# Attention on one core: normalization one query tile later, transposes two and the product with V three tiles behind the scores

## The chip, the cores and the metric

The kernel runs on one core of one Trainium2 chip. The metric is the device time of one execution in microseconds, as the median of several executions; lower is better.

## What is computed

The reference is causal attention with a second, linear "memory" part, followed by two dense blocks without bias. Cut to what matters:

```
B, H, S, D = 4, 8, 576, 64
scores = q @ k.T / sqrt(D); scores[j > i] = -1e9
a      = exp(scores - scores.max(-1)); a /= a.sum(-1) + 1e-9
local  = a @ v
q_p    = phi(q)                         # q+1 where q>0, else exp(q)
mem    = (q_p @ M_prev) / (q_p . z_prev + 1e-6)
x      = sigmoid(beta) * mem + (1 - sigmoid(beta)) * local     # (2304, 512)
x      = ((x @ w1) * (x @ w2)) @ w3 @ w_out                    # d_ff 1024
h      = x @ w_in                                              # d_ff 2048
out    = (h - tanh(h)) @ w_out2
```

The weights arrive as 64-bit numbers; the kernel loads the raw words and decodes them on the chip to float32, and then splits each into a high and a low part for TensorE (three matmuls in place of one).

## The kernel before

**Attention.** 32 heads are taken as 16 pairs P. Each pair has five query tiles u: four of 128 rows and a fifth of 64 rows in which both heads share the 128 partitions. That makes 80 tiles, n = 0 to 79, with n = 5P + u. A tile goes through five steps, each a function:

- S, `scores` and `rmax`: the score matmuls of the causal part (width 128(u+1); 288 twice for u = 4) and the mask matmuls on TensorE into a PSUM tile `sc`, of which there are two; then the row maximum on VectorE (L337) into the small tile `st`.
- E, `exps`: the exponential on ScalarE (L346) with its row sum; it frees the `sc` tile.
- N, `norm`: 1e-9 is added (L355) and the reciprocal is taken (L356) on VectorE, then the rows are scaled on GpSimd (L363).
- T, `trans`: the scaled rows are transposed on TensorE, block by block (L395, L402, L406), and copied out of PSUM to the `g` tiles (L374 on ScalarE or L376 on VectorE).
- A, `av`: for u = 1 and u = 4 the product with V, `o<-g,v` on TensorE; the result is copied to `xs`. After u = 4 the V of the pair after next is loaded (L189).

Two more letters stand in the loop: L loads and scales the next pairs' q and k, and G runs background work: first `fold_work`, the product of w3 and w_out, in 16 groups of 12 matmuls `fo` whose operands are decoded by a chain of steps (L74 on ScalarE; L75, L77, L81, L84 on VectorE; L96 and L99 on GpSimd); the two halves of a result are added on VectorE (L257) and split (L259 on ScalarE, L260 on VectorE). After the folds come the first w1 and w2 tiles (`wa`, `wb`) and the memory part (`mem_tok`: tiles `mw` with L490, L491, L493, L494, L497 and so on, transposes L506, product `mo`, sum L523).

**What sets the order.** A loop over m calls the steps in the order of the string ORDER, each for tile m minus its lag:

```python
ORDER = "SENTLGA"
for m in range(NU + 8):
    for x in ORDER:
        do(x, m - LAG[x])
```

This is the order of issue. A scheduler then lays the instructions of each engine in a row, with its own estimates of when each could start, and the order of issue counts where several could go. So each engine's row differs from the order of issue, and a lag moves what may be chosen rather than a fixed place. Each engine then runs its row in order. Buffers are given in the order of issue.

**After attention.** The tiles of attention are given back (`att.close()`), and new pools take their place, among them the one that holds w1 and w2 from the third pair on. Then six groups g of 384 tokens go through the first dense block: `ab<-xh,wa` and `ab<-xh,wb` (24 matmuls for each of eight slices f), ScalarE and VectorE (L646, L647, L650, L651), and `x<-abh,wf`. The decoding of the remaining weights and the rest of the memory part run beside the first groups. The second dense block (`h`, `o<-...,gh`) ends the kernel.

Of the kernel before, what the change touches and what calls it, by code (L numbers as in the profile page):

```python
# [32 lines left out]
def block_kernel(ctx, tc, qk, qt, vt, mp, zp_d, beta, w1, w2, w3t, wo, wi, wo2, ident_d, mask_d, out):  # L33
# [104 lines left out]
    def run(gen):  # L138
        for _ in gen:
            pass  # L140
# [17 lines left out]
    DW = 1  # L158
    HIP = 1
    ORDER = "SENTLGA"  # L160
    LAG = {'S': 0, 'E': 0, 'N': 0, 'T': 1, 'L': 0, 'G': 3, 'A': 2}
    WI = ()
    PO_, PA = "xzw", "r1234"
    OP, FL = 5, "V"
# [99 lines left out]
    if True:  # L264
# [170 lines left out]
        N = 384  # L435
# [135 lines left out]
        def do(x, n):  # L571
            if not 0 <= n < NU:
                return
            P, u = units[n]
            if x == "S":
                scores(n)
                rmax(n)
            elif x == "E":
                exps(n)
            elif x == "N":  # L580
                norm(n)
            elif x == "T":
                trans(n)
            elif x == "A" and u in (1, 4):
                av(P, u // 4)
                if u == 4 and P + 2 < 16:
                    load_v(P + 2)
            elif x == "L":
                if u == 0 and 1 <= P <= 16 - RB:
                    load_qk(P + RB - 1)  # L590
                if u == 2 and P < 15:
                    scale_q(P + 1)
            elif x == "G":
                bgc[0] += BG if n < MB else BG2
                with ExitStack() as s:
                    for e, k in TH:
                        if n - k >= 0:
                            s.enter_context(tc.issue_after(mark[e][n - k]))
                    while bgc[0] >= 1:
                        if next(bg, None) != 1:  # L600
                            bgc[0] -= 1
# [4 lines that stand above are left out]
        run(bg)  # L606
# [308 lines left out]
def build(nc, arrays):  # L915
    args = []
    for name, a in arrays.items():
        args.append(nc.dram_tensor(f"in_{name}", a.shape, mybir.dt.from_np(a.dtype), kind="ExternalInput").ap())
    o = nc.dram_tensor("out_0", (_N, 512), F32, kind="ExternalOutput").ap()
    with tile.TileContext(nc, schedule_with_timeline_sim=True) as tc:  # L920
        block_kernel(tc, *args, o)
# [40 lines left out]
```

## Time and profile before

| | |
|---|---|
| median of 3 executions | 1037.43 us (1036.61 to 1040.4) |
| the profiled execution's own time | 1034.81 us |
| its span, first to last instruction | 1033.0 us |
| TensorE busy | 984.2 us (95%) |
| VectorE busy | 745.9 us (72%) |
| ScalarE busy | 594.7 us (58%) |
| GpSimd busy | 361.8 us (35%) |
| mean granted TensorE clock | 0.990 |

A busy share is an average over stages with different limits: the attention tiles run from the start to about 275 us, the first dense block from there to about 620 us, the second to the end. Which engine limits a stage is read from that stage.

### The profile page before, as it was taken

How to read it: one execution, taken by the hardware profiler on the slowest of the kernel's cores; microseconds unless marked ns; L12 is line 12 of the kernel's file. 1: busy time of each engine (PE TensorE's matmuls, PEld its weight loads, DVE VectorE, ACT ScalarE, POOL GpSimd, SP SyncE). 2: the span in 40 equal slices, each digit the busy share in tenths (PEclk: the TensorE clock that was granted, in tenths of full speed). 3: DMA queues.
4: the chain of work that ended last, by engine and by line, in shares of the span. 5: the costliest groups of instructions: out<-in, count | busy, mean ns of one | idle time of the engine just before them, and what ended most of it. 6: DMA issues, size and time to landing. Idle time of an engine off the chain costs nothing.

```text
span 1033.0 us, 15587 instructions
## 1 busy us (share of the span) xinstructions
PE 984.2 (95%) x5512; PEld 826.1 (80%) x5512; DVE 745.9 (72%) x1361; ACT 594.7 (58%) x1356; POOL 361.8 (35%) x396
## 2 busy tenths in 40 slices
PE   5999999889988989999999979999999999999998
PEld 2565566545777878999999979999999999989996
DVE  5858787787599996475212497778787887788775
ACT  4767766577433433233222546777686676777765
POOL 3656655585466213200000573322222222222221
PEclk9999999999999999999999998999999999999999
DMA  6434543242145552143000010000000000000000
GB/s 206 158 113 128 177 139 98 97 144 88 42 135 156 160 184 81 34 134 109 1 1 1 1 62 1 1 1 31 1 32 1 1 32 1 29 4 1 32 1 31
DMA packets 44238, 68.27 MB, mean 66 GB/s; under 512 B 4865, under 2 KB 30209, under 8 KB 44161
## 3 DMA queue, kind: packets, MB, share of 16 engines
q1 hardware_dynamic: 44160, 67.29, 20.4%
q8 instruction: 43, 0.70, 0.3%
q14 instruction: 35, 0.28, 0.1%
HBM read 62.56 MB, written 4.72 MB: 65 GB/s over the span
## 4 chain that ended last, share of the span: by engine, by line
PE 79%; DVE 11%; issue 3%; DMA 3%; ACT 2%; POOL 2%; SPq 0%; DVEq 0%; ACTq 0%; POOLq 0%
PE o L143 24%; PE h L143 20%; PE ab L143 14%; PE x L143 7%; PE sc L143 6%; PE fo L143 4%; PE t L395 3%; DVE T L81 2%; DVE T L75 2%; DVE st L337 1%; PE mo L143 1%; DVE T L77 1%; ACT p L346 1%; DMA raw<-in_wi 1%; DVE T L84 1%
## 5 line engine op out<-in xcount | busy, mean ns | idle before, releaser
L849 POOL TENSOR_TENSOR gl<-s,gh 128x384 fp32r<-128x384 f32 x96 | 100.8, 1050 | 292.3 <-ACT gh L843 281.7
L363 POOL TENSOR_SCALAR p<-p,st 128x128 f32<-128x128 f32 (+2 forms) x144 | 94.5, 669 | 63.4 <-DVE st L356 32.3
L143 PE MATMUL x<-abh,wf 128*128 128x384 f32 x384 | 109.1, 345 | 5.6 <-ACT abh L650 5.6
L143 PE MATMUL ab<-xh,wa 128*128 128x384 f32 x384 | 109.3, 342 | 4.4 <-POOL wa L99 2.1
L143 PE MATMUL ab<-xh,wb 128*128 128x384 f32 x384 | 108.3, 340 | 3.1 <-POOL wb L96 2.0
L825 DVE SCALAR_TENSOR_TENSOR s<-s,u 128x384 f32<-128x384 f32 x96 | 81.9, 853 | 21.8 <-ACT s L815 20.7
L143 PE MATMUL sc<-r 64*64 64x288 f32 (+4 forms) x384 | 79.6, 480 | 17.5 <-ACT p L346 11.7
L346 ACT ACTIVATE p<-sc,st 128x128 f32<-128x128 f32 (+2 forms) x144 | 78.3, 549 | 29.8 <-DVE st L337 25.1
L647 DVE TENSOR_TENSOR a<-ab,a 128x384 f32<-128x384 f32 x48 | 26.4, 551 | 86.3 <-PE ab L143 73.5
L74 ACT ACTIVATE T<-raw 128x512 f32<-128x512 f32 x72 | 48.6, 674 | 62.3 <-DMA raw<-in_wi 11.9
L821 ACT ACTIVATE u<-u,pc 128x384 f32<-128x384 f32 x96 | 59.3, 619 | 43.4 <-DVE s L825 43.3
L337 DVE TENSOR_REDUCE st<-sc 128x2 f32<-128x256 f32 (+4 forms) x80 | 64.1, 803 | 26.6 <-PE sc L143 26.2
L831 DVE TENSOR_TENSOR t<-h,t 128x384 f32<-128x384 f32 x96 | 53.3, 555 | 38.8 <-ACT t L814 38.5
L143 PEld LDWEIGHTS ab<-xh,wa 128*128 128x128 f32 x384 | 70.3, 188 | 9.0 <-issue 3.1
L143 PEld LDWEIGHTS x<-abh,wf 128*128 128x128 f32 x384 | 71.3, 192 | 7.1 <-ACT abh L650 6.5
L143 PEld LDWEIGHTS ab<-xh,wb 128*128 128x128 f32 x384 | 71.1, 190 | 4.6 <-POOL wb L96 2.8
L813 ACT ACTIVATE u<-h 128x384 f32<-128x384 f32 x96 | 47.0, 490 | 48.0 <-PE h L143 48.0
L143 PE MATMUL x<-abl,wf 128*128 128x384 f32 x192 | 67.0, 349 | 5.5 <-DVE abl L651 5.5
L830 DVE SCALAR_TENSOR_TENSOR s<-s,s 128x384 f32<-128x384 f32 x96 | 61.0, 635 | 8.1 <-DVE s L825 0.5
L143 PE MATMUL ab<-xl,wa 128*128 128x384 f32 x192 | 65.1, 339 | 0.0
L143 PE MATMUL ab<-xl,wb 128*128 128x384 f32 x192 | 64.7, 337 | 0.0
L837 DVE COPY_PREDICATED s<-u,t 128x384 f32<-128x384 uint32 x96 | 58.6, 610 | 8.3
(218 smaller groups left out, 2579.5 us busy)
## 6 DMA issues: line engine op xcount, KB each, us to landing
raw<-in_wo SPq DMA_DIRECT2D x24, 512.0 KB, 3.5
r<-in_qk SPq DMA_DIRECT2D x15, 576.0 KB, 4.1
raw<-in_w3t SPq DMA_DIRECT2D x16, 512.0 KB, 3.7
raw<-in_w SPq DMA_DIRECT2D x16, 512.0 KB, 3.7
raw<-in_wi SPq DMA_DIRECT2D x16, 512.0 KB, 3.8
v<-in_vt SPq DMA_DIRECT2D x16, 320.0 KB, 3.1
mw<-in_qt SPq DMA_DIRECT2D x18, 256.0 KB, 2.9
out<-ob SPq DMA_DIRECT2D x18, 256.0 KB, 2.3
```

The costliest lines, as they stand in the source:

```text
L74: AC.activation(out=tf, in_=hw.bitcast(F32), func=AF.Abs)
L143: return PE.matmul(o, lhsT, rhs, start=start, stop=stop).ins
L337: mark["V"][n] = DV.tensor_reduce(out=st[:, 0:2] if u < 4 else st[:, 0:1], in_=seen(n), axis=AX.X if u < 4 else AX.XY, op=ALU.max, negate= ...
L346: mark["A"][n] = AC.activation(out=p[:, x], in_=sc[:, x], func=AF.Exp, bias=st[:, x.start:x.start + 1], accum_out=st[:, 2 + x.start:3 + x. ...
L363: (DV if NV[u] == "V" else PO).tensor_scalar(out=pr, in0=pr, scalar1=sc, scalar2=1.0, op0=ALU.mult, op1=ALU.mult)
L813: AC.activation(out=u, in_=o, func=AF.Square)
L821: AC.activation(out=u, in_=u, func=AF.Relu, bias=pc[:, 2:3])
L825: DV.scalar_tensor_tensor(out=s1, in0=s1, scalar=k2[0], in1=u, op0=ALU.add, op1=ALU.mult)
L830: DV.scalar_tensor_tensor(out=s1, in0=s2, scalar=k2[1], in1=s1, op0=ALU.add, op1=ALU.mult)
L831: DV.tensor_tensor(out=t, in0=o, in1=t, op=ALU.subtract)
L837: DV.copy_predicated(out=s1, mask=u[:].bitcast(U32), data=t)
L849: PO.tensor_tensor(out=l, in0=s1, in1=h[:].bitcast(F32), op=ALU.subtract)
```

## The change

One line differs: the lags of N, T and A each grow by one. Normalization of a tile is issued one step after its scores and exponential, the transposes two steps after, and the product with V three steps after. The lags of the loads and of the background work stay.

```diff
     ORDER = "SENTLGA"
-    LAG = {'S': 0, 'E': 0, 'N': 0, 'T': 1, 'L': 0, 'G': 3, 'A': 2}
+    LAG = {'S': 0, 'E': 0, 'N': 1, 'T': 2, 'L': 0, 'G': 3, 'A': 3}
```

Every engine runs the same instructions as before, in the same number. Of TensorE's 5178 rows the first 78 (to the mask of tile 7 and a few transposes) and the last 3387 (from inside the first dense block on) stand in the same order as before; in between tiles trade places. Two places show how.

**Place A, the end of the last fold.** On VectorE, around the sum L257 of the last fold, before (the reduction at the end is that of tile 57; `sc_2209` is its score tile, `sc_2146` that of tile 56):

```order
L257 TENSOR_TENSOR s_2178<-fo_2165,wf7p_1356 128x512
L337 TENSOR_REDUCE st_2151<-sc_2146 128x2
L493 SCALAR_TENSOR_TENSOR mw_2184<-mw_2184 128x512
L81 SCALAR_TENSOR_TENSOR T_2193<-raw_2187,T_2193 128x512
L260 TENSOR_TENSOR wf7_2180<-s_2178,wf7_2180 128x512
L337 TENSOR_REDUCE st_2214<-sc_2209 128x2
```

and after the change (`sc_2187` is tile 57, `sc_2225` tile 58):

```order
L257 TENSOR_TENSOR s_2169<-fo_2156,wf7p_1335 128x512
L260 TENSOR_TENSOR wf7_2171<-s_2169,wf7_2171 128x512
L337 TENSOR_REDUCE st_2192<-sc_2187 128x2
L81 SCALAR_TENSOR_TENSOR T_2207<-raw_2180,T_2207 128x512
L497 TENSOR_REDUCE mst_2310<-mw_2175 128x8
L376 COPY g1_2082<-t_2147 128x8x64
L337 TENSOR_REDUCE st_2230<-sc_2225 128x2
```

The reduction of tile 56, a step of the memory part and a decode step no longer stand between the last fold's sum and the reduction of tile 57. On TensorE, from the last matmuls of that fold on, before (128x256 is tile 56, 128x384 tile 57):

```order
L143 MATMUL fo<-wb_1408,zs 128x512 x3
L143 MATMUL sc<-r 128x256 x2
L143 LDWEIGHTS identb
L143 MATMUL sc<-maskb,identb 128x128
L143 LDWEIGHTS identb
L143 MATMUL sc<-maskb,identb 128x128
L143 MATMUL sc<-r 128x384 x2
```

and after (128x512 is tile 58):

```order
L143 MATMUL fo<-wb_1399,zs 128x512 x3
L143 MATMUL sc<-r 128x384 x2
L143 LDWEIGHTS identb
L143 MATMUL sc<-maskb,identb 128x128
L395 MATMUL t<-ident,p 128x128 x4
L143 LDWEIGHTS identb
L143 MATMUL sc<-maskb,identb 128x128
L143 MATMUL sc<-r 128x512 x2
```

The last fold moved behind the scores of tile 56, one tile later. The first fold moved likewise, behind the scores of tile 10 in place of tile 9.

**Place B, the end of attention.** On TensorE the last product with V, `o<-g,v`, before (the `ab` matmuls are the first two slices of the dense block, and 12 of them stand behind the product, ahead of the transposes L506):

```order
L143 MATMUL ab<-xh,wb_2653 128x384 x2
L143 MATMUL ab<-xl,wb_2653 128x384
L143 MATMUL ab<-xh,wb_2653 128x384
L143 MATMUL o<-g_2884,v_102 64x320 x6
L143 MATMUL o<-g_2884,v_102 64x192 x2
L143 MATMUL o<-g_2885,v_102 64x64 x2
L143 MATMUL ab<-xh,wa_2391 128x384
L143 MATMUL ab<-xl,wa_2391 128x384
```

and after:

```order
L143 MATMUL ab<-xh,wb_2640 128x384
L143 MATMUL ab<-xl,wb_2640 128x384
L143 MATMUL ab<-xh,wb_2640 128x384
L143 MATMUL o<-g_2894,v_102 64x320 x6
L143 MATMUL o<-g_2894,v_102 64x192 x2
L143 MATMUL o<-g_2895,v_102 64x64 x2
L143 MATMUL mo<-ident,mw 128x128 x4
```

All 48 `ab` matmuls of the two slices now stand ahead of the last product. On ScalarE the copy of that product, `xs<-o,omgt` of 128x5x64, before:

```order
L374 ACTIVATE xs_1685<-o,omgt 128x5x64
L646 ACTIVATE a<-ab 128x384 x2
L650 ACTIVATE abh<-a 128x384
L374 ACTIVATE mq_1534<-mo 128x2x128
L74 ACTIVATE T<-raw 128x512
```

and after:

```order
L646 ACTIVATE a<-ab 128x384 x2
L650 ACTIVATE abh<-a 128x384 x2
L374 ACTIVATE xs_1717<-o,omgt 128x5x64
L374 ACTIVATE mq_1513<-mo 128x2x128
L74 ACTIVATE T<-raw 128x512
```

The steps of the first two slices moved ahead of the copy; the next decode step L74 stays behind both.

## Rows read from the trace of the kernel before

**Rows 1.** Windows by stage: busy us (instructions) by engine, granted clock, DMA share, GB/s.
```profile
30.00:200.00 170.00, 167.17 (x1068) 100.46 (x1067) 126.81 (x276) 115.47 (x319) 100.27 (x134) 1.00 0.40 126
200.00:275.00 75.00, 66.69 (x465) 38.63 (x466) 57.89 (x138) 50.41 (x141) 46.15 (x60) 0.98 0.32 104
275.00:400.00 125.00, 111.33 (x621) 98.08 (x621) 111.10 (x206) 45.43 (x90) 50.66 (x42) 0.96 0.46 144
400.00:600.00 200.00, 200.00 (x1166) 196.20 (x1165) 88.60 (x166) 64.90 (x133) 28.36 (x24) 1.00 0.15 44
```

**Rows 2.** Timeline of all engines, 194 to 222: start, duration, instruction, [idle before].
```profile
194.81 0.69 DVE L257 TENSOR_TENSOR s<-fo,wf7p 128x512 f32<-128x512 f32 x1 [0.72 <-PE fo L143]
...
195.54 0.63 ACT L259 ACTIVATE wf<-s 128x512 fp32r<-128x512 f32 x1 [0.46 <-DVE s L257]
195.56 0.92 PE L143 MATMUL sc<-r 64*128 64x384 f32 x4
...
197.04 1.65 POOL L494 TENSOR_TENSOR mw<-mw,mc 128x512 f32<-128x512 f32 x1 [2.06 <-DVE mw L493]
...
197.50 1.75 DVE L260 TENSOR_TENSOR wf<-s,wf 128x512 fp32r<-128x512 f32 x1
197.53 1.13 PE L143 MATMUL sc<-r 64*128 64x512 f32 x4 [0.28 <-ACT p L346]
...
198.71 0.39 PE L395 MATMUL t<-ident,p 128*128 128x128 f32 x2
...
199.17 0.94 DVE L337 TENSOR_REDUCE st<-sc 128x2 f32<-128x768 f32 x1
...
200.78 0.57 ACT L346 ACTIVATE p<-sc,st 128x384 f32<-128x384 f32 x1
...
201.49 1.19 PE L143 MATMUL sc<-r 64*64 64x288 f32 x8 [2.40 <-ACT p L346]
...
202.74 4.11 PE L143 MATMUL o<-g,v 128*64 128x320 f32 x20
```

**Rows 3.** The window behind that wait, columns as in rows 1.
```profile
201.50:206.70 5.20, 5.20 (x29) 2.47 (x29) 4.81 (x13) 1.66 (x5) 2.82 (x5) 0.67 0.52 153
```

**Rows 4.** Chain that ended last: a product of the same 20 matmuls, later.
```profile
234.84 2.35 PE o L143 x20
```

**Rows 5.** Instructions of L260: duration ns min/median/max, first and last start.
```profile
L260 DVE TENSOR_TENSOR wf<-s,wf x8: 677/722/1748, 140.2 to 197.5; 128x512 fp32r<-128x512 f32 x8
```

**Rows 6.** Timeline of TensorE at the end of attention.
```profile
275.62 2.42 PE L143 MATMUL o<-g,v 128*64 128x320 f32 x20
277.97 0.45 PE L143 MATMUL ab<-xh,wa 128*128 128x384 f32 x1
...
279.99 0.33 PE L143 MATMUL ab<-xh,wb 128*128 128x384 f32 x1
```

**Rows 7.** Timeline of GpSimd, same stretch.
```profile
278.22 0.62 POOL L96 TENSOR_SCALAR wa<-T 128x512 fp32r<-128x512 f32 x1 [4.39 <-PE o L143]
```

**Rows 8.** Timeline of ScalarE, same stretch.
```profile
278.09 0.53 ACT L374 ACTIVATE xs<-o,omgt 128x320 f32<-128x320 f32 x1 [4.69 <-PE o L143]
...
281.08 0.65 ACT L74 ACTIVATE T<-raw 128x512 f32<-128x512 f32 x1
```

**Rows 9.** Timeline of VectorE, same stretch.
```profile
279.39 0.56 DVE L647 TENSOR_TENSOR a<-ab,a 128x384 f32<-128x384 f32 x1 [5.15 <-ACT a L646]
...
282.61 0.41 DVE L75 TENSOR_SCALAR T<-T 128x512 f32<-128x512 f32 x1
282.94 0.55 DVE L651 TENSOR_TENSOR abl<-a,abh 128x384 fp32r<-128x384 f32 x1
...
283.74 0.41 DVE L490 TENSOR_SCALAR mw<-mw 128x512 f32<-128x512 f32 x1
```

**Rows 10.** Waits of VectorE, 255 to 400: us in total, times, longest.
```profile
DVE mw L490 <- DMA mw<-in_qt: 6.5, 4, 3.0
```

**Rows 11.** DMA issues of the page: times, KB each, us to landing.
```profile
v<-in_vt SPq DMA_DIRECT2D x16, 320.0 KB, 3.1
```

**Rows 12.** Transposes of TensorE: duration ns min/median/max, first and last start.
```profile
L395 PE MATMUL t<-ident,p x320: 270/273/476, 16.9 to 268.3; 128*128 128x128 f32 x160
```

## The prediction

> **What bounds the kernel now.** I read the windows by stage first [rows 1]. From 30 to 200 us, the larger part of attention, TensorE is busy 167.17 of 170 us: all other engines fit beside it, and no change of order can save more there than the 2.83 us that are left. From 200 to 275, after the last fold, there is no background matmul to fill in and TensorE is busy 66.69 of 75: 8.31 us of waits. From 275 to 400 TensorE waits 13.67 us, now for decoded weights, and VectorE is the engine with the least room, 111.10 of 125. From 400 to 600 TensorE does not stop at all. So the change can act where it moves instructions, between about 30 and 380 us, and the reader should see that only some 11 us of TensorE waits lie inside attention, and that a shift of VectorE's work at 280 is passed on, since TensorE waits for that work until about 400.
>
> **What the change leaves alone.** The instructions and their number are the same, so no engine gains or loses work. The first 78 rows of TensorE stand as before, so the waits of the start stay. Buffers: the rows `p` have one tile for each u, needed again five tiles later, and the transposes that free it move from one step behind to two; three steps are left, so I cost this at nothing. Its cover is those three steps; gone, it would be a wait of ScalarE for a transpose. The `st` tiles are six, enough for one step more. The V load is issued with the product, one step later; it lands in 3.1 us [rows 11] and is first used ten tiles later, more than 30 us, so it too costs nothing, and on the load queue it passes at most a few loads. Between 30 and 200 the moved tiles trade places under a full TensorE; the one spot in doubt is the first fold, now behind the scores of tile 10. Those scores lose 12 fold matmuls as cover, while the exponential of tile 8 that they wait for also stands earlier on ScalarE. I take zero; the bounds are a gain of the 2.83 us above and a loss of one wait like the longest of this kind, 2.40 us [rows 2].
>
> **Place A, the last fold.** In the trace before, TensorE reaches tile 59 at 198.71 + 0.39 = 199.10 us and starts it at 201.49, having waited 2.40 us for the exponential of tile 57 [rows 2]. The chain behind that wait is VectorE's row: the fold's sum L257 at 194.81, then four instructions, L260 among them for 1.75 us, and only at 199.17 the reduction of tile 57. From the start of that reduction to the start of tile 59 it is 201.49 - 199.17 = 2.32 us.
>
> After the change VectorE does L257 as soon as the fold ends, ScalarE L259 (done 195.54 + 0.63 = 196.17, which is 1.4 us after the fold), VectorE L260, and then the reduction at once. With L260 at its median of 0.72 [rows 5] the reduction starts 2.1 us after the fold and tile 59 may start at 4.4; with L260 at 1.75 it may start at 5.5. TensorE gets there after tiles 57 and 58 and their transposes: before this took 199.10 - 195.56 - 0.28 = 3.3 us, and there are two transposes more, so 3.5 us. The wait is then 0.9 to 2.0 us in place of 2.40, a gain of 1.5 to 0.4. I take 0.9, the middle, since L260 lies at either end depending on what GpSimd does beside it: its 1.75 us fell on GpSimd's L494 of 197.04 to 198.69 [rows 2].
>
> The Trainium skill ("SBUF — State Buffer", section "Who interferes with whom") says that a VectorE instruction with two inputs in SBUF contends with a GpSimd instruction that reads SBUF; the trace agrees, 1.75 against 0.72 us. By that rule L260 is slow wherever a scaling or a split of GpSimd lies beside it, as is likely after the change too, and the gain would be 0.4: the sum below would end 0.5 us higher, at 1036.6.
>
> Behind the wait of 2.40 the granted clock fell to 0.67 over 201.5 to 206.7 [rows 3], a mean of full and half speed, and the product there took 4.11 us [rows 2] against 2.35 for the same 20 matmuls later [rows 4]: 1.76 us. Whether the clock still falls behind a wait of 0.9 to 2.0 us the rows do not say; the bounds are 0 and a gain of 1.76, and I take half, 0.9.
>
> **Place B, the end of attention.** The first weights whose place is freed by the end of attention are split on GpSimd (L96), which waits 4.39 us for the last product with V [rows 7]. Twelve `ab` matmuls that stood behind that product now stand ahead of it: from 277.97 to 279.99 + 0.17 is 2.19 us [rows 6], so the product, L96, L99 and with them the next free decode tile and L74 (281.08 before [rows 8]) come about 2.2 us later, at some 283.3. In the other direction ScalarE no longer holds the first two slices behind the copy of that product, for which it waited 4.69 us [rows 8]; VectorE had waited 5.15 us for it [rows 9]. VectorE's L490 waits for a load that landed by 283.74 in any case, and stands ahead of L75 after the change, so L75 starts at about 284.1 in place of 282.61, 1.5 us late, while L651 (0.55) and L490 (0.41), which had followed L75, are done by then [rows 9]. The net is 1.5 - 0.96 = 0.5 us, on the engine that TensorE waits for next. The bounds are 0 (all of it made good) and 2.2 (none).
>
> **The sum.** Against the profiled execution's 1034.81 us: - 0.9 - 0.9 + 0.5 = 1033.5. The median of the three runs shown lies 2.62 us above that execution, so the same step gives 1036.1 for a median. The ends are - 1.5 - 1.76 + 0 and - 0.4 + 0 + 2.2 on the three terms, 1034.2 to 1039.2; with the first fold's loss of 2.4 the upper is 1041.6.
>
> **The rivals.**
> 1. *The tiles without background work stop waiting altogether.* With everything behind the exponential issued later, VectorE could take each reduction at once, and the 8.31 us of 200 to 275 [rows 1] and the slow product's 1.76 would go: 1037.43 - 10.1 = 1027.4. For it speaks that these waits are for the exponential and for copies. Against it: from tile 59 on the rows of TensorE and VectorE are nearly the same as before, tile for tile, so what waits there now will go on waiting.
> 2. *The end of attention is late and decides.* In place B the 2.2 us are not made good, the load that L490 waits for adds its longest wait, 3.0 us [rows 10], now ahead of L75, and TensorE's longer wait is followed by another slow stretch, 1.76: 1037.43 + 7.0 = 1044.4. It is slower by over 0.5% only if all three links hold (2.2 + 3.0 is 5.2). For it: VectorE is the tight engine there. Against it: the load is issued when L506 is done, which does not move.
> 3. *The lag does little.* The scheduler already set normalization and transposes behind the next tiles' scores, so the order of issue was not what held them: 1037.4.
> 4. *TensorE is not full in attention.* Waits could hide inside its records. Weight loads are busy 100.46 of 170 us there, against 196.20 of 200 later [rows 1]. If work issued earlier could bring that stretch to the ratio of 275 to 400, 98.08 to 111.33, it would take 114 us in place of 167 and the kernel about 984. Against it: the transposes, which the change moves, have a median of 273 ns and a shortest of 270 [rows 12], so nothing hides in them. The Trainium skill ("Perfetto Trace Analysis", section "Identifying the Most-Contended Engine") says that busy time of matmuls is a bad measure of headroom and that of weight loads a good one; by that rule this rival would be the likely one, and the transposes' rows do not bear it out.
>
> **How the numbers follow.** The measurement of this kernel tells about 0.5%, some 5.2 us, from no change. Chances: my sum 0.48, rival 3 0.17, rival 2 0.18, rival 1 0.15, rival 4 0.02. My sum and rival 3 lie within 0.5%: 0.65. Rivals 1 and 4 are faster: 0.17. Rival 2 is slower: 0.18. The predicted time is 1036.1. The range is 1029 to 1045: it takes in rival 2 at its price and most of the way to rival 1, and leaves out rival 4 and the ends of rivals 1 and 2, about 0.16. My sum's own range is 1034 to 1041.6.
>
> **What would show it.** Right: TensorE busy in 30 to 200 at about 98% as before; tile 59 starting within 2 us of the transposes ahead of it; the first L96 behind the last product about 2 us later, counted from the scores of tile 79; the waits of tiles 60 to 79 as they were. Wrong: TensorE's waits between 200 and 275 near zero (rival 1), VectorE waiting 3 us at L490 near 283 with L75 behind it (rival 2), or a wait of TensorE between 30 and 60 that is not there now. A different number of slow-clock stretches between 275 and 400 would shift the time by about 1.7 us each without any of my steps being wrong.

## The result and the profile after

The changed kernel takes 1045.54 us (median of 12 executions, 1039.99 to 1050.77) against 1038.01 for the kernel before in the same comparison: a ratio of 1.0065, 95% interval 1.0049 to 1.0081. It is slower by 0.65%, some 6.7 us. The prediction was 1036.1 with a range of 1029 to 1045 and 0.65 on no change, so the forecast was wrong, and the time lies just above the range.

The profiled execution took 1045.53 us (span 1043.7). The windows by stage of the changed kernel, columns as in [rows 1]:

```profile
30.00:200.00 170.00, 164.40 (x1043) 98.78 (x1042) 129.13 (x270) 114.56 (x316) 95.84 (x132) 1.00 0.40 126
200.00:275.00 75.00, 64.48 (x447) 35.92 (x446) 59.39 (x136) 48.55 (x140) 43.28 (x61) 0.95 0.32 101
275.00:400.00 125.00, 111.78 (x628) 96.55 (x626) 111.43 (x202) 45.75 (x91) 50.95 (x42) 0.97 0.44 140
400.00:600.00 200.00, 198.13 (x1146) 194.28 (x1146) 82.68 (x165) 61.68 (x127) 24.28 (x21) 0.99 0.14 44
```

The first row is the one to look at. TensorE waits 5.60 us between 30 and 200 where it waited 2.83 [rows 1]: the stretch that I had called full, where moved tiles could only trade places. The last query tile, 79, starts its scores at 263.10 us in place of 255.92, so in these two profiles attention alone ends 7.18 us later. From 30 us to that start TensorE is busy 218.23 of 233.10 us against 215.51 of 225.92 before: of the loss, 14.87 - 10.41 = 4.46 us are waits, and 2.72 us are longer busy time for the same matmuls. The clock is the larger part of the 2.72. Before, TensorE ran at half clock (1.2 in place of 2.4 GHz) from 202.8 to 206.2 us; after the change it did so up to 31.2 us, and from 236.0 to 242.8 (the first row is before, the second after):

```profile
202.80:206.20 3.40, 3.40 (x15) 1.66 (x16) 3.40 (x12) 1.45 (x4) 2.32 (x4) 0.50 0.66 200
236.00:242.80 6.80, 5.58 (x25) 2.78 (x25) 5.32 (x15) 4.28 (x14) 3.47 (x5) 0.50 0.34 109
```

If half of the busy time at half clock is lost, an estimate from these rows, that is 1.70 us before, and 2.79 + 0.60 = 3.39 after (0.60 for the 1.2 us from 30 us on). So some 1.7 us of the 2.72 are the clock; the other 1.0 us lies at full clock.

**Where the new waits are.** The timeline of TensorE in the changed kernel shows a wait ahead of the scores of tiles 44, 49, 54 and 59, each the fifth tile of its pair (64x288); before, only tile 59 waited. This is one of them, tile 49, with all that leads to it (start, duration, instruction, [idle before]):

```profile
162.97 0.92 PE L143 MATMUL sc<-r 64*128 64x384 f32 x4
163.08 0.69 DVE L257 TENSOR_TENSOR s<-fo,wf3p 128x512 f32<-128x512 f32 x1
163.81 0.63 ACT L259 ACTIVATE wf<-s 128x512 fp32r<-128x512 f32 x1 [1.21 <-DVE s L257]
163.99 1.32 POOL L99 TENSOR_TENSOR zs<-T,zs 128x512 fp32r<-128x512 f32 x1
164.31 0.28 PE L143 MATMUL sc<-maskb,identb 128*128 128x128 bf16 x2
164.47 1.39 DVE L260 TENSOR_TENSOR wf<-s,wf 128x512 fp32r<-128x512 f32 x1 [0.28 <-ACT wf L259]
164.52 1.13 PE L143 MATMUL sc<-r 64*128 64x512 f32 x4
165.78 0.94 DVE L337 TENSOR_REDUCE st<-sc 128x2 f32<-128x768 f32 x1
166.14 0.27 PE L406 MATMUL t<-ident,p 128*64 128x128 f32 x1
166.82 0.58 ACT L346 ACTIVATE p<-sc,st 128x384 f32<-128x384 f32 x1 [1.71 <-DVE st L337]
...
168.11 1.19 PE L143 MATMUL sc<-r 64*64 64x288 f32 x8 [1.69 <-ACT p L346]
...
187.64 1.19 PE L143 MATMUL sc<-r 64*64 64x288 f32 x8 [0.88 <-ACT p L346]
```

Read it from the bottom. Tile 49 waits for the exponential of tile 47, whose PSUM tile it needs. That waits for tile 47's row maximum at 165.78, although its scores were complete at 164.31 + 0.28 = 164.59. In between VectorE held the fold's subtraction L260, which stands ahead of the maximum, had to wait for ScalarE's L259, and took 1.39 us. Meanwhile TensorE had only tile 48's scores and some transposes to do, and stood still from 166.42 on. This is the chain of place A, which I had described for the last fold and tile 59 [rows 2]. The change brings the same chain to two earlier folds, ahead of tiles 49 and 54. At tile 44, which waits 0.55 us, VectorE takes the maximum ahead of the subtraction, so there it is only that TensorE has too little to do. In the kernel before, the same place reads (tile 47's maximum, the product with V, and tile 49, which waits for nothing):

```profile
159.02 0.94 DVE L337 TENSOR_REDUCE st<-sc 128x2 f32<-128x768 f32 x1
163.53 2.42 PE L143 MATMUL o<-g,v 128*64 128x320 f32 x20
166.47 0.70 PE L143 MATMUL sc<-r 64*64 64x288 f32 x4
```

TensorE's row shows why. The last eight groups of twelve `fo` matmuls stood behind the scores of tiles 40, 42, 45, 47, 50, 52, 54, 55; after the change they stand behind 39, 41, 44, 46, 49, 51, 54, 56. So a group stands behind the second tile of a pair (46) in place of the third (47), and the sum and the subtraction come on VectorE just as the third tile's scores are ready. And the product with V (2.42 us) that stood between the fourth tile's scores and the fifth's now stands behind the fifth's.

**Place A** after the change (timeline, columns as above; 128x768 is tile 57, the wait is that of tile 59):

```profile
201.74 0.66 DVE L257 TENSOR_TENSOR s<-fo,wf7p 128x512 f32<-128x512 f32 x1
203.10 0.69 DVE L260 TENSOR_TENSOR wf<-s,wf 128x512 fp32r<-128x512 f32 x1 [0.70 <-ACT wf L259]
203.71 0.95 DVE L337 TENSOR_REDUCE st<-sc 128x2 f32<-128x768 f32 x1
206.04 1.19 PE L143 MATMUL sc<-r 64*64 64x288 f32 x8 [1.41 <-ACT p L346]
207.54 2.42 PE L143 MATMUL o<-g,v 128*64 128x320 f32 x20
...
236.71 0.42 PE L406 MATMUL t<-ident,p 128*64 128x128 f32 x1 [2.66 <-DVE g L376]
239.13 4.23 PE L143 MATMUL o<-g,v 128*64 128x320 f32 x20
```

The wait of 2.40 [rows 2] is 1.41, inside the predicted 0.9 to 2.0, and the product behind it runs at its full speed, 2.42 us where it had taken 4.11. But a wait of 2.66 us, for a copy of a transposed block, stands at 236.71, and there a product takes 4.23. The window behind it shows the clock:

```profile
235.00:243.00 8.00, 5.78 (x25) 2.78 (x25) 6.32 (x15) 4.28 (x14) 4.67 (x7) 0.57 0.42 130
```

This wait lies behind the scores of tile 69, and the kernel before has it too, with 1.25 us. What differs can be read in VectorE's row. After the change a step L75 of the background's decoding stands directly ahead of tile 68's maximum and of the copy that TensorE waits for; before, the maximum came first. After, then before:

```profile
233.74 1.18 DVE L75 TENSOR_SCALAR T<-T 128x512 f32<-128x512 f32 x1
234.84 1.21 DVE L337 TENSOR_REDUCE st<-sc 128x2 f32<-128x1024 f32 x1
235.98 0.67 DVE L376 COPY g<-t 128x512 f32<-128x512 f32 x1
```

```profile
231.03 1.22 DVE L337 TENSOR_REDUCE st<-sc 128x2 f32<-128x1024 f32 x1
233.57 0.30 PE L406 MATMUL t<-ident,p 128*64 128x128 f32 x1 [1.25 <-DVE g L376]
```

**Place B**, the end of attention (timeline):

```profile
287.49 0.62 POOL L96 TENSOR_SCALAR wa<-T 128x512 fp32r<-128x512 f32 x1 [7.16 <-PE o L143]
...
289.98 0.68 ACT L74 ACTIVATE T<-raw 128x512 f32<-128x512 f32 x1 [1.66 <-POOL wa L99]
290.58 0.90 DVE L490 TENSOR_SCALAR mw<-mw 128x512 f32<-128x512 f32 x1 [1.80 <-DMA mw<-in_qt]
291.40 0.41 DVE L75 TENSOR_SCALAR T<-T 128x512 f32<-128x512 f32 x1
```

Counted from the scores of tile 79, L96 comes at 287.49 - 263.10 = 24.39 us against 278.22 - 255.92 = 22.30 [rows 7], 2.09 later, and L75 at 28.30 against 26.69 [rows 9], 1.61 later: 2.2 and 1.5 had been predicted. In these two profiles the last `ab` matmul ends 629.15 - 263.10 = 366.05 us behind tile 79's start, against 617.1 - 255.92 = 361.18, as if the end of attention cost 4.9 us. The experiments show that it does not.

### The profile page after: what moved, and what is told of

Its sections match the earlier page's. It is cut to its first block, busy times and chain, and to the rows that moved or that the text cites. A ratio compares the mean times of both kernels' runs of the same rounds, so it can differ in the third digit from the quotient of the medians.

```text
span 1043.7 us, 15583 instructions
## 1 busy us (share of the span) xinstructions
PE 988.1 (95%) x5512; PEld 828.2 (79%) x5512; DVE 754.6 (72%) x1361; ACT 594.4 (57%) x1356; POOL 358.4 (34%) x396
## 3 DMA queue, kind: packets, MB, share of 16 engines
HBM read 62.56 MB, written 4.72 MB: 64 GB/s over the span
## 4 chain that ended last, share of the span: by engine, by line
PE 76%; DVE 14%; issue 3%; ACT 3%; DMA 2%; POOL 2%; SPq 0%; DVEq 0%; ACTq 0%; POOLq 0%
PE o L143 23%; PE h L143 19%; PE ab L143 15%; PE x L143 7%; PE sc L143 4%; PE fo L143 4%; DVE st L337 2%; PE t L395 2%; DVE T L81 2%; DVE T L75 2%; DVE T L77 2%; ACT p L346 1%; DMA mw<-in_qt 1%; PE mo L143 1%; DVE T L84 1%
## 5 line engine op out<-in xcount | busy, mean ns | idle before, releaser
L363 POOL TENSOR_SCALAR p<-p,st 128x128 f32<-128x128 f32 (+2 forms) x144 | 89.5, 635 | 69.9 <-DVE st L356 40.0
L74 ACT ACTIVATE T<-raw 128x512 f32<-128x512 f32 x72 | 48.6, 676 | 54.5 <-DMA raw<-in_wi 13.4
```

Of the source, the lines that this page charges most:

```text
L74: AC.activation(out=tf, in_=hw.bitcast(F32), func=AF.Abs)
L363: (DV if NV[u] == "V" else PO).tensor_scalar(out=pr, in0=pr, scalar1=sc, scalar2=1.0, op0=ALU.mult, op1=ALU.mult)
```

## The experiments

Three theories stood after the two traces were read. **F**: the fold groups' new places cost, through waits of the fifth tiles. **B**: the end of attention costs, through the later decoding. **T**: the later transposes and products cost by themselves, wherever the folds stand. No run has the lag of N alone, so its share is not shown. In the expectations "recurrence products" are the `ab` matmuls, and ACT is ScalarE. All ratios are to the kernel before on the same chip.

**1. One lag alone.** The transposes' lag (the diff shown), and in a second kernel the product's (`'T': 1`, `'A': 3`):

```diff
-    LAG = {'S': 0, 'E': 0, 'N': 0, 'T': 1, 'L': 0, 'G': 3, 'A': 2}
+    LAG = {'S': 0, 'E': 0, 'N': 0, 'T': 2, 'L': 0, 'G': 3, 'A': 2}
```

> Transposes two tiles behind the scores, everything else as before (the product with V stays at two). The groups of twelve fold products stand where they stood before up to query tile 42 and partly move after that (tiles 46, 48, 52, 54, 55, 56, 58 in place of 45, 47, 50, 52, 53, 54, 55); the last product with V stands behind 48 recurrence products as in the changed kernel. Theory F (the fold groups' new places uncover the scores of the tiles with five keys' blocks): about half of the loss, 1041 us. Theory B (the last product behind more recurrence products): the end's loss alone, about 1041 us. Theory T (the transposes' own lateness costs, wherever folds stand): all of the loss, 1045 us.

> Product with V three tiles behind, transposes one behind as before. Folds and the end's order as in the changed kernel. Theories F and B: as the changed kernel, 1045 us, with the same score waits for ACT's exponentials between 140 and 210 us. Theory T: as before, 1038 us.

Measured: transposes alone 1042.54 us, 1.0061 (1.0042 to 1.0079); product alone 1043.01, 1.0067 (1.0042 to 1.0093). Each by itself costs about what both cost, which no theory of added delays gives. The time of the second speaks against T. The traces of both lack the chain of tile 49, which speaks against waits of the fifth tiles as the whole of F. With the transposes alone no fifth tile waits between 130 and 210 us; tile 79 starts at 260.20, and the waits are others, among them three of 0.93 to 1.35 us in which a product waits for the transposed rows that are now late for it:

```profile
98.69 2.16 PE L143 MATMUL o<-g,v 128*64 128x320 f32 x16 [1.35 <-DVE g L376]
```

With the product alone the folds stand as in the changed kernel, but VectorE takes the third tile's maximum ahead of the subtraction, and tiles 44, 49 and 54 wait 0.55 us each, where the waits of the changed kernel had been expected:

```profile
165.76 0.96 DVE L337 TENSOR_REDUCE st<-sc 128x2 f32<-128x768 f32 x1
167.46 0.67 DVE L260 TENSOR_TENSOR wf<-s,wf 128x512 fp32r<-128x512 f32 x1
168.10 1.19 PE L143 MATMUL sc<-r 64*64 64x288 f32 x8 [0.55 <-ACT p L346]
```

The profiled execution is the fastest of its seven, 1038.49 us, so what makes the others slower is not in this trace.

**2. The background's lag moved along, or moved alone.** The second kernel is the first one's mirror image: the lags of before with `'G': 2`.

```diff
-    LAG = {'S': 0, 'E': 0, 'N': 1, 'T': 2, 'L': 0, 'G': 3, 'A': 3}
+    LAG = {'S': 0, 'E': 0, 'N': 1, 'T': 2, 'L': 0, 'G': 4, 'A': 3}
```

> The changed kernel's three lags, with the background's lag 4 in place of 3: the groups of fold products and the last product stand as before, relative to the scores. Theories F and B: 1038 us (within 2 us of before), no score wait for ACT of over 0.8 us between 100 and 200 us. Theory T: 1045 us.

> The three lags of before, with the background's lag 2 in place of 3: the fold groups and the last product stand as in the changed kernel. Theories F and B: 1045 us, with waits of scores for ACT as in the changed kernel. Theory T: 1038 us.

Measured: the changed lags with the folds put back 1036.11 us, 0.9993 (0.9982 to 1.0005); the lags of before with the folds moved 1045.45, 1.0084 (1.0069 to 1.0098). The whole loss is there without the change's lags and gone with them, so T falls as the cause of the change's loss. What moved is the whole background, the folds' decode steps with the folds. In the first kernel the groups from tile 25 to 54 stand exactly as before; five early groups and the last stand one or two tiles later.

**3. One part of attention at a time.** The lags change at tile 65: those of the change behind it (`LAG_B`, "late end"), or ahead of it ("early end").

```diff
+    LAG_A, LAG_B, SWITCH = {'N': 0, 'T': 1, 'A': 2}, {'N': 1, 'T': 2, 'A': 3}, 65
...
-                do(x, m - LAG[x])
+                for n in range(NU):
+                    if n + {**LAG, **(LAG_B if n >= SWITCH else LAG_A)}[x] == m:
+                        do(x, n)
+                if x == "G" and m - LAG["G"] >= NU:
+                    do(x, m - LAG[x])
```

> The lags of before for tiles 0 to 64, those of the change for tiles 65 to 79. All sixteen groups of fold products stand as before, the last product with V stands behind 47 recurrence products in place of 36 (48 in the changed kernel). Theory B (the end of attention costs by itself): 1039.5 to 1041.5 us, 3 to 5 over before. Theory F (the fold groups' places alone cost): 1036.5 us, as before.

> The lags of the change for tiles 0 to 64, those of before for tiles 65 to 79. The fold groups stand as in the changed kernel, the last product with V stands behind 35 recurrence products, as before. Theory F: the attention part of the loss, 1040 to 1043.5 us, tile 79 starting 4 to 7 us later than before. Theory B: 1036.5 us, as before.

Measured: late end 1039.34 us, 1.0009 (0.9995 to 1.0024); early end 1043.16, 1.0056 (1.0041 to 1.007). So what the change does up to tile 64 is worth 5.8 us (4.3 to 7.3), and what it does behind it 0.9, with -0.5 to 2.5 as its interval: B is not clear of zero. Together they are 6.7, what the change costs. In the profile of the late end the order of the changed kernel gives the same delays (POOL and DVE, timeline):

```profile
281.15 0.62 POOL L96 TENSOR_SCALAR wa<-T 128x512 fp32r<-128x512 f32 x1 [7.07 <-PE o L143]
284.15 0.99 DVE L491 TENSOR_SCALAR mw<-mw 128x512 f32<-128x512 f32 x1 [1.71 <-DMA mw<-in_qt]
285.06 0.41 DVE L75 TENSOR_SCALAR T<-T 128x512 f32<-128x512 f32 x1
```

The step L96 is 281.15 - 256.77 = 24.38 us behind tile 79's start, as in the changed kernel, and the wait of L490 (here L491) for its load is there too. The last `ab` then ends 363.55 us behind that start. In the early end, whose order at this place is that of before, it is 364.28, later and not earlier. A single profile differs there by 3 to 4 us from one kernel to the next for other reasons: over the profiles of this study the last `ab` ends 361.18 to 365.09 us behind tile 79's start in the five kernels whose last product stands behind 36 `ab` (mean 363.4), and 362.79 to 366.05 in the seven where it stands behind 48 (mean 364.2). The 4.9 us above can't be put on place B.

**4. The background one step later still.** The lags of before with `'G': 4`, and those of the change with `'G': 5`:

> The three lags of before, with the background's lag 4 in place of 3: the last product stands behind 28 recurrence products in place of 36, and the late fold groups end one tile later than before (43, 45, 48, 50, 53, 55, 58 in place of 42, 45, 47, 50, 52, 54, 55). Theory B: the end comes earlier, 1 to 3 us faster than before from that place. Theory F: the groups that are now behind tiles 43, 48, 53 and 58, the tiles just ahead of the fifth ones, cover these as well as before, so no loss in attention; if not, 2 to 4 us slower.

> The three lags of the change, with the background's lag 5 in place of 3: folds and last product as in the kernel with the lags of before and a background lag of 4. If only the order between background and scores counts, the same time as that kernel within 2 us; if the lags themselves cost, up to 7 us more.

Measured: 1041.99 us, 1.0044 (1.0028 to 1.0059), and 1035.67, 0.9987 (0.9978 to 0.9997). That the order of folds and scores alone counts is refuted here: the groups end behind the same tiles in both and the last product behind the same 28 `ab`, and yet there are 5.9 us between them. With folds this late the change's lags help. The first kernel is slower than before, where B expected it to be faster, and it is so without any wait of a fifth tile over 0.3 us. In the profiles 4.99 of 5.98 us at the start of tile 79 are longer busy time of the same matmuls (217.69 against 212.70 us since 30 us), not waits. Some 1.7 us of that is the clock: the first kernel ran at 0.51 from 231.8 to 235.2, the second has no such stretch there. What slows the rest was not settled.

**5. Early folds or late folds.** In the changed kernel the background's lag is 4 for its first 25 steps and 3 after them; the second kernel has 3 first and 4 after them.

```diff
+    GLAG = lambda n: 4 if n < 25 else 3
...
-                do(x, m - LAG[x])
+                if x == "G":
+                    for n in range(NU + 8):
+                        if n + GLAG(n) == m:
+                            do(x, n)
+                else:
+                    do(x, m - LAG[x])
```

> The lags of the change, the background's lag 4 for its first 25 steps and 3 after them. The early fold groups stand about as in the kernel with lag 4 throughout, the late ones (from tile 34 on) and the last product as in the changed kernel. If the late groups carry the loss: 1042 to 1045.5 us. If the early ones do (the first group, behind tile 10): 1037 us.

> The reverse: lag 3 for the background's first 25 steps, 4 after them. Early fold groups as in the changed kernel, late ones and the last product (behind 36 recurrence products) as before. If the late groups carry the loss: 1036 to 1038 us, and no wait of the 64x288 scores for ACT over 0.8 us at 148, 168 and 187 us. If the early ones do: 1042 us or more.

Measured: late folds as in the change 1046.81 us, 1.009 (1.0072 to 1.0109), a little above what was expected; late folds as before 1035.31, 0.9978 (0.9965 to 0.9992). The first fold behind tile 10, my one spot in doubt, stands there in both and costs nothing. The folds from tile 34 on, with the background behind them, carry the loss. The timeline of the second kernel (its lines behind L161 are one higher) at the same place:

```profile
158.15 0.92 PE L143 MATMUL sc<-r 64*128 64x384 f32 x4
160.00 0.94 DVE L338 TENSOR_REDUCE st<-sc 128x2 f32<-128x768 f32 x1
162.61 1.13 PE L143 MATMUL sc<-r 64*128 64x512 f32 x4
163.89 0.67 DVE L258 TENSOR_TENSOR s<-fo,wf3p 128x512 f32<-128x512 f32 x1
164.11 2.42 PE L143 MATMUL o<-g,v 128*64 128x320 f32 x20
165.39 0.68 DVE L261 TENSOR_TENSOR wf<-s,wf 128x512 fp32r<-128x512 f32 x1
165.99 1.21 DVE L338 TENSOR_REDUCE st<-sc 128x2 f32<-128x1024 f32 x1
167.05 1.19 PE L143 MATMUL sc<-r 64*64 64x288 f32 x8
```

Tile 47's maximum (160.00) is done before the fold's sum (163.89) exists; the maximum that now stands behind the subtraction is tile 48's, which tile 50 needs, and the product of 2.42 us covers it. Tile 49 waits for nothing. Neither does tile 59 (201.12, behind its transposes and a product), and this kernel has the lowest ratio of the study. Its profile doesn't show that this is the gain of place A: a wait of 2.30 us for ScalarE comes at 211.75, ahead of tile 63, with half clock behind it, and TensorE's idle time up to tile 79 is 11.00 us against 10.41 before.

**6. The subtraction off VectorE.** The changed kernel, and as a control the one before, with L260 on GpSimd:

```diff
-    OP, FL = 5, "V"
+    OP, FL = 5, "P"
```

> The changed kernel with the subtraction L260 of each fold on GpSimd in place of VectorE; fold groups on TensorE stand as in the changed kernel. If the row maximum of the third tile of a pair being held behind L260 makes the waits of the 64x288 scores: the maximum starts about 1.1 us earlier, the wait of 1.69 us near 168 falls under 0.7, those of 0.55 and 0.88 near 149 and 188 go, and the kernel gains 2 to 4 us on the changed one, 1041.5 to 1043.5. If it is only that TensorE has too little work between (the product with V stands behind these scores and not ahead), the waits stay above 1 us at 168 and the time at 1045.

> The kernel of before with L260 on GpSimd. Its folds stand elsewhere, so only tile 59 waits behind L260 (2.40 us): 0.5 to 1.5 us there, and the kernel within 2 us of before; slower by up to 3 us if GpSimd's scaling of the rows becomes late by the 1.3 us that it takes over.

Measured: the changed kernel 1039.05 us, 1.0017 (0.9999 to 1.0035); the control 1036.17, 0.9988 (0.9975 to 1.0001). Of the change's 6.7 us some 5.0 are gone (2.5 to 7.5, by the two intervals), where the control gains 1.2 (-0.1 to 2.6). The folds stand as in the changed kernel, and the same place reads:

```profile
162.30 0.68 DVE L257 TENSOR_TENSOR s<-fo,wf3p 128x512 f32<-128x512 f32 x1
163.80 0.28 PE L143 MATMUL sc<-maskb,identb 128*128 128x128 bf16 x2
164.12 0.96 DVE L337 TENSOR_REDUCE st<-sc 128x2 f32<-128x768 f32 x1 [0.74 <-PE sc L143]
165.16 1.73 POOL L260 TENSOR_TENSOR wf<-s,wf 128x512 fp32r<-128x512 f32 x1
166.46 1.19 PE L143 MATMUL sc<-r 64*64 64x288 f32 x8 [0.54 <-ACT p L346]
```

Now the maximum waits for the scores and not the other way, and the wait of 1.69 us is 0.54. The waits of tiles 44, 54 and 59 read 0.55 each. I had expected those of 0.55 and 0.88 to go, and 0.55 is what stays: that much is the thin cover on TensorE, the product behind these scores. The four waits are shorter by (0.55 + 1.69 + 0.88 + 1.41) - (0.55 + 0.54 + 0.55 + 0.55) = 2.34 us, so they do not explain all of the 5.0. The rest of what this profile wins on the changed kernel's lies behind the folds: between 200 us and tile 79 TensorE waits 5.77 us in place of 9.27, the wait of 2.66 and the slow product do not come, and the clock from 30 us to tile 79 is 1.00 in place of 0.98. How those follow from the subtraction's move is not shown.

The kernels beside each other, from their profiles (tile 79's start; TensorE's idle time from 30 us to it, and in 120 to 200) and their timed runs:

| kernel | tile 79 | idle to it | 120:200 | ratio |
|---|---|---|---|---|
| before | 255.92 | 10.41 | 1.22 | |
| changed | 263.10 | 14.87 | 3.66 | 1.0065 |
| lags of before, folds moved (2) | 263.86 | 16.70 | 6.15 | 1.0084 |
| early end (3) | 262.02 | 15.77 | 4.72 | 1.0056 |
| late folds as in the change (5) | 260.63 | 13.95 | 3.20 | 1.0090 |
| late end (3) | 256.77 | 10.02 | 1.17 | 1.0009 |
| changed lags, folds put back (2) | 254.56 | 11.41 | 0.82 | 0.9993 |
| late folds as before (5) | 255.25 | 11.00 | 0.79 | 0.9978 |
| L260 on GpSimd (6) | 255.65 | 9.76 | 1.67 | 1.0017 |
| before, L260 on GpSimd (6) | 255.38 | 10.09 | 0.55 | 0.9988 |
| product alone (1) | 258.96 | 13.76 | 2.94 | 1.0067 |
| transposes alone (1) | 260.20 | 13.83 | 1.97 | 1.0061 |
| lags of before, background one later (4) | 258.40 | 10.71 | 1.74 | 1.0044 |
| changed lags, background two later (4) | 252.42 | 9.72 | 1.65 | 0.9987 |

The idle time in 120 to 200 separates the kernels whose late folds stand as in the change (2.9 to 6.2 us) from those whose late folds stand as before (under 1.3); moving L260 brings it to 1.67 with the folds where the change puts them. The last three rows, whose folds stand in a third and a fourth way, don't fit this: idle times of 1.65 to 1.97 go with a gain and with two losses. The profiles of "late folds as in the change" and "product alone" are of the fastest execution of their kernels, 1040.47 us of a median of 1046.81 and 1038.49 of 1043.01, so their rows show less than their ratios.

## Why the prediction was wrong

**The step that failed** is "Between 30 and 200 the moved tiles trade places under a full TensorE", costed at zero but for the first fold, with 2.40 us as the bound of a loss. The rows of TensorE showed 2.83 us of idle time [rows 1], and I read from that only how much there was to win. A full engine says nothing of how much there is to lose: it was full because of where each fold and each product with V stood; before, tiles 44, 49 and 54 wait for nothing. It cost 5.8 us. The bound was wrong for the same reason: I allowed one wait of that kind. There were three new ones, at tiles 44, 49 and 54 (3.12 us together, two of them through the subtraction), a longer one at tile 69 (2.66 for 1.25), and more time at half clock. Two more steps of the prediction fell with it: "the waits of tiles 60 to 79 as they were" (9.27 us from 200 us to tile 79, against 7.58), and the 0.9 us taken for the slow product behind tile 59's wait were won there and lost again behind tile 69's, where a product takes 4.23 us.

**What is shown of the cause.** That the late folds' new places carry the loss is shown by experiments 2, 3 and 5. That it acts through the subtraction ahead of the maximum is shown for the changed kernel by experiment 6, in part: 2.5 to 7.5 of 6.7 us, of which 2.34 can be seen in the waits. It is not the only way: the product's lag alone puts the folds in the same places, has the maximum ahead of the subtraction, and costs as much.

**The material was there.** I had worked out the chain at tile 59 from the trace, sum, subtraction, maximum, exponential, scores, and had looked in the order only at the first and the last fold for where it would stand. The order between them showed the maximum of the third tile behind L257 and L260 at the folds behind tiles 46 and 51, before anything ran. What was named as a sign of being right, TensorE at about 98% in 30 to 200, is 164.40 of 170, 96.7%.

**Place A** was right at its place: the wait is 1.41 us, the slow product behind it is gone. As a term of the sum it is not shown: the changed kernel has a slow product at 239.13 in its stead. The kernel with late folds as before (experiment 5) gains some 2.3 us (0.8 to 3.6) where 1.8 were taken for the two terms, but its profile has a new wait and a slow stretch at 211.75, so the agreement may be luck.

The Trainium skill ("SBUF — State Buffer", section "Who interferes with whom") says that a VectorE instruction with two inputs in SBUF contends with a GpSimd instruction that reads SBUF. The changed kernel agrees: L260 took 1.39 us beside GpSimd's L99 at 164.47, and 0.69 at 203.10, when GpSimd was idle from 203.24 to 208.35. I had weighed this rule at one fold only; by it, the slow L260 belongs to each fold that has a split beside it.

**Place B** was right in its delays (2.09 and 1.61 us), and its price of 0.5 with bounds of 0 to 2.2 is not contradicted: measured 0.9 with an interval of -0.5 to 2.5, too wide to tell it from nothing.

**The rivals.** Rival 2's time, 1044.4, is nearest to the result, but not for its reason: the load's wait at L490 came (1.80 us), and yet the end of attention costs about 1 us; that the numbers meet is luck. Rival 1 did not come: TensorE waits 10.52 us in 200 to 275, not less. Rival 3 holds for the lags themselves in one respect, since with the folds put back the kernel is within 0.1% of before. Rival 4 is not borne out: where the change's time moved, it moved for the most part by waits and clock. What would show the prediction wrong was named as a wait between 30 and 60; the longest there is 0.97 us at 47.22, in place of one of 0.82 at 46.51, and the new waits came between 148 and 207.

**What stays open.** Why, besides the clock, 217.69 us of matmul time in experiment 4 became 212.70 with other lags. How much of the 5.8 us is the lower clock: some 1.7 us in the changed kernel's profile, none in that of the early end, which spends as long at half clock as the kernel before (239.4 to 242.8) and has all of its loss in waits and 0.74 us of busy time. Why the product's lag alone costs as much as the change without the chain. And whether the wait at 236.71, which lies behind the background's decoding, comes from the folds or only from the background that moved with them.

## What to carry to other kernels

An engine that is full tells how little a change of order can win there, and nothing of what it can lose: for each moved block of filler work, look which short instructions it brings with it onto the other engines, and whose turn it takes there. When a chain of waits has been found at one place, search the new order for every other place where the same sequence now stands. When a lag is changed in a loop of several lags, the lag of the filler work belongs to the change: it moved by a tile though its own number did not.

## What the runs showed of the hardware

In the changed kernel's profile TensorE's waits of 0.55 to 1.69 us in 140 to 210 were not followed by a lower clock: behind the wait of 1.41 the granted clock was

```profile
206.00:212.00 6.00, 5.96 (x48) 3.22 (x48) 5.62 (x15) 4.17 (x12) 3.57 (x5) 1.00 0.61 192
```

while the wait of 2.66 us, with another of 0.52 behind it, was followed by 0.57 over 235 to 243, a mean of time at 2.4 and at 1.2 GHz, as the one of 2.40 was by 0.67 in the kernel before [rows 3]. A single wait thus cost its own length and, in the two long ones, 1.7 to 1.8 us more in the product that followed (4.11 and 4.23 against 2.42). The length of the wait does not decide it alone: waits of 1.06, 0.62 and 1.48 us from 218 to 223 were not followed by the low clock in the changed kernel, and waits of 1.05, 0.62 and 1.47 us at the same tiles were, with 0.50 from 225.9 to 229.3, in the kernel with the lags of before and the folds moved.
